# A chunked linear recurrence and a dense feed-forward layer in one kernel: the decay of C moves to the rows, three kinds of small matmuls get visits of their own, and GpSimd keeps the selects

## The chip, the core and the metric

The kernel runs on one core of a Trainium2 chip. The time is device microseconds of one execution. Several executions are timed, and the median is compared. A core has five engines with instruction queues of their own: PE (TensorE, matmuls, with weight loads listed as PEld), DVE (VectorE), ACT (ScalarE), POOL (GpSimd) and SP (SyncE, which issues the DMAs here). They meet through semaphores.

## The reference

Four batches, eight heads, 768 tokens, head dimension 32, state size 16. The first part is a recurrence over chunks with decay `a`, the second a two-matrix layer with a softplus between.

```python
for c in range(nc):                       # per chunk of tokens
    cum = np.cumsum(log_a[chunk], axis=-1)
    L = np.exp(cum[:, None] - cum[None, :]) * causal
    M = (Cc @ Bc.T) * L                   # scores
    y = M @ xc + (Cc @ state) * exp(cum)  # values + read
    state = exp(sum(la)) * state + sum_j Bc[j] * xc[j] * exp(cum[-1] - cum[j])
h = y @ w_in                              # (3072, 256) x (256, 2048)
g = softplus(h)
out = g @ w_out                           # (3072, 2048) x (2048, 256)
```

The weights arrive as 64-bit floats and are turned into 32-bit ones on the chip.

## The kernel before, in words

Tokens are taken in six rounds `r` of 128 tokens of each of the four batches, 512 columns in all. The six rounds of the recurrence feed the six column blocks `j` of the layer. All work is written out by hand: the string `ORDER` is a list of words, each of which emits the instructions of one step, and every engine keeps that order (`InOrder`). All instructions come through one helper, so the profile gives them one line, L141; they are told apart by their tiles.

The words of a round are these. `S` (scores) are 32 matmuls of B against C; a matmul of 32-bit data is two records, so 64 in the trace. `sel`, `rmp` (POOL) and `rm` (DVE) write the masked decay factors into `rm`; `M` multiplies the scores into it. `I` (values) is 64 matmuls, 128 records, of `rm` with x. `U` (updates, 64 records) makes the outer products for the state, `D`/`DD` keep their diagonal blocks in `zm`, `T` and `N` carry the state on. `R` (read, 64 records) adds C times state into the banks that `I` began. `G` (DVE) multiplies the result, in PSUM, by the growth tile `gg`, giving `y` in SBUF; `Xa` (ACT) rounds it to `xh`, `Yv`/`Yp` form the rest `xl`. `gg` of rounds 1 to 5 comes from DRAM (`gd`), each as four DMAs; that of round 0 is made on PE and ACT (`gs`, `ge`). `Bv`/`Bp` and `Cv`/`Cp` scale B and C by factors.

The layer's words are `F:j,k` (first matrix, six matmuls of 512 columns into bank 2 or 3), `s` (softplus, ACT, which empties that bank), `ha`/`hv`/`hp` (the rounded part `gh`, on ACT, DVE or POOL), `l` (the rest `gl`, DVE) and `Z:j,k` (second matrix, six matmuls). There are 96 `F` and 96 `Z`; I call either a block. Sixteen weight tiles `p` are loaded (`w:p`) and converted before they are needed: `Wg` (rebias, tile `w`), `Ws` or `Wsv` (sign), `Wb` and `Wo`, or `Wbv` and `Wo` (bits and word), `Wh` (high part), `Wl` (low part). Here `Wg`, and some of `Wh`, `Wl`, `h`, `T`, `N`, `B` and `C`, run on POOL.

Columns 0 and 1 are begun together: `F:0,0` starts when round 0 is through, round 1 and the weights are prepared beside the blocks of columns 0 and 1, and `F:2,0` follows round 2. From there a fixed pattern repeats, one round of the recurrence to one column. In it rounds 3 and 4 have one visit of PE, between `Z:j,6` and the next `F`:

```
F:2,10,2 Z:2,6 U:4,4,6 I:3,4,6,0,4 R:3,4,6,0,4 s:2,10 ha:2,10 l:2,10 F:2,11,3 Z:2,7 ...
```

and round 5, which has no `U` after it, `F:4,10,2 Z:4,6 I:5,4,6,0,4 R:5,4,6,0,4`. The DMAs are issued by SP in the same order; a DMA that waits holds back those after it.

## Time and profile before

| | us |
|---|---|
| timed runs, median (lowest to highest of 3) | 342.81 (341.96 to 346.05) |
| profiled execution, its own time | 344.31 |
| its span, first to last instruction | 342.6 |
| PE busy | 310.8 |
| DVE, ACT, POOL busy | 169.7, 135.5, 81.8 |
| mean granted clock of PE, share of full speed | 0.965 |

The span is what the views below are made of; 1.7 us of the execution's time lie outside it. A busy PE is a PE with matmuls under way, and records overlap, so that the time of a block is read from the distance of starts, not from durations.

### The profile page before, as it was taken

What the parts mean: (1) busy time and instruction counts of PE and PEld (TensorE: products, weight loads), DVE (VectorE), ACT (ScalarE), POOL (GpSimd) and SP (SyncE); (2) the same over time, 40 slices, a digit from 0 to 9 for tenths busy, and PEclk for the clock granted to TensorE, in tenths of its full rate; (3) what the DMA queues carried; (4) which work ended last, traced back from release to release, by engine and by line L of the source; (5) the groups of instructions that cost most, each with busy time, mean ns of one, the idle gap of its engine ahead of it and who ended that gap; (6) DMA issues with size and microseconds to landing.
All of it is one profiled execution on the core that took longest, in us unless ns stands there. A gap on an engine that the chain in (4) does not pass through costs nothing.

```text
span 342.6 us, 7297 instructions
## 1 busy us (share of the span) xinstructions
PE 310.8 (91%) x3148; PEld 253.8 (74%) x3148; DVE 169.7 (50%) x244; ACT 135.5 (40%) x228; POOL 81.8 (24%) x88
## 2 busy tenths in 40 slices
PE   5649879899799992999989999989999999999995
PEld 4538568678688781878868878868878888888884
DVE  4629979979796338336207325207335234232222
ACT  4625564323432212344415444405444434454440
POOL 5846972726712014500060000060000000000000
PEclk9958999999999998799989999989999999999999
DMA  7946323721540402041032031002010000010001
GB/s 228 388 174 186 104 87 120 279 66 58 231 106 2 146 11 61 0 138 51 0 97 61 3 121 65 0 4 61 2 61 2 0 4 1 0 61 3 0 0 61
DMA packets 14432, 26.05 MB, mean 76 GB/s; under 512 B 1088, under 2 KB 6976, under 8 KB 13760
## 3 DMA queue, kind: packets, MB, share of 16 engines
q1 hardware_dynamic: 14400, 25.60, 22.4%
q8 instruction: 24, 0.39, 0.5%
q14 instruction: 8, 0.07, 0.1%
HBM read 22.35 MB, written 3.24 MB: 75 GB/s over the span
## 4 chain that ended last, share of the span: by engine, by line
PE 77%; DVE 10%; issue 6%; POOL 3%; ACT 2%; DMA 1%; SPq 0%; DVEq 0%; ACTq 0%
PE banks L141 77%; DVE w L141 4%; DVE gl L141 2%; POOL w L141 1%; ACT e L141 1%; POOL xl L141 1%; DVE rm L141 1%; POOL cc L141 1%; DMA lr<-in_logs 1%; DVE s L141 1%; DVE y L141 0%; DVE zm L141 0%; ACT gh L141 0%; DVE bp L141 0%; ACT xh L141 0%
## 5 line engine op out<-in xcount | busy, mean ns | idle before, releaser
L141 DVE TENSOR_TENSOR gl<-e,gh 128x512 fp32r<-128x512 f32 x96 | 67.9, 716 | 136.7 <-ACT gh L141 129.6
L141 ACT ACTIVATE e<-banks 128x512 f32<-128x512 f32 x96 | 57.1, 597 | 110.1 <-PE banks L141 88.4
L141 PE MATMUL banks<-xh,wih 128*128 128x512 f32 (+1 forms) x196 | 78.9, 403 | 4.2 <-ACT xh L141 4.2
L141 PE MATMUL banks<-xl,wih 128*128 128x512 f32 (+1 forms) x196 | 77.7, 397 | 3.0 <-POOL xl L141 2.0
L141 PE MATMUL banks<-gh,woh 128*128 128x512 f32 (+1 forms) x196 | 76.9, 392 | 1.7 <-DVE half L141 1.7
L141 PE MATMUL banks<-xh,wil 128*128 128x512 f32 (+1 forms) x196 | 77.5, 395 | 0.0
L141 PE MATMUL banks<-gl,woh 128*128 128x512 f32 (+1 forms) x196 | 76.6, 391 | 0.8 <-DVE gl L141 0.8
L141 PE MATMUL banks<-gh,wol 128*128 128x512 f32 (+1 forms) x196 | 76.3, 389 | 0.6 <-DVE wol L141 0.6
L141 ACT CAST gh<-e 128x512 fp32r<-128x512 f32 x79 | 48.8, 619 | 52.3 <-PE banks L141 52.2
L141 POOL TENSOR_SCALAR_AFFINE_SELECT rm<-fc 64x1024 f32<-64x1024 f32 (+1 forms) x26 | 30.5, 1173 | 82.6 <-PE banks L141 81.5
L141 PEld LDWEIGHTS banks<-xh,wih 128*128 128x128 f32 x196 | 38.2, 195 | 13.2 <-ACT xh L141 4.6
L141 PEld LDWEIGHTS banks<-xl,wih 128*128 128x128 f32 x196 | 38.3, 196 | 10.7 <-POOL xl L141 2.3
L141 PEld LDWEIGHTS banks<-gh,woh 128*128 128x128 f32 x196 | 37.5, 192 | 10.0 <-DVE half L141 2.1
L141 PEld LDWEIGHTS banks<-gl,woh 128*128 128x128 f32 x196 | 37.5, 192 | 9.0 <-DVE gl L141 1.5
L141 PEld LDWEIGHTS banks<-xh,wil 128*128 128x128 f32 x196 | 38.2, 195 | 7.7
L141 PEld LDWEIGHTS banks<-gh,wol 128*128 128x128 f32 x196 | 37.5, 191 | 8.6 <-DVE wol L141 1.0
L141 POOL TENSOR_SCALAR w<-wraw 128x512 f32<-128x512 f32 x10 | 15.8, 1583 | 20.1 <-DVE wil L141 8.6
L141 DVE SCALAR_TENSOR_TENSOR w<-w,s 128x512 int32<-128x512 int32 x16 | 17.9, 1124 | 4.6 <-POOL w L141 4.1
L141 PE MATMUL banks<-rm,toks 64*32 64x64 f32 x768 | 10.2, 233 | 7.1 <-issue 5.3
L141 POOL CAST gh<-e 128x512 fp32r<-128x512 f32 x12 | 8.8, 743 | 28.9 <-PE banks L141 24.4
L141 DVE TENSOR_TENSOR rm<-banks,rm 128x1024 f32<-128x1024 f32 (+1 forms) x14 | 14.7, 1064 | 1.6 <-POOL rm L141 1.6
L141 PEld LDWEIGHTS banks<-rm,toks 64*32 64x32 f32 x768 | 8.6, 108 | 8.5 <-issue 6.1
(71 smaller groups left out, 192.4 us busy)
## 6 DMA issues: line engine op xcount, KB each, us to landing
rows<-in_rows SPq DMA_DIRECT2D x5, 1024.0 KB, 5.6
wraw<-in_w_in SPq DMA_DIRECT2D x8, 512.0 KB, 4.7
wraw<-in_w_out SPq DMA_DIRECT2D x8, 512.0 KB, 3.5
toks<-in_toks SPq DMA_DIRECT2D x5, 768.0 KB, 6.0
out_t<-half SPq DMA_DIRECT2D x11, 256.0 KB, 2.1
gg<-gd SPq DMA_DIRECT2D x20, 128.0 KB, 3.0
rows<-in_rows SPq DMA_DIRECT2D x1, 512.0 KB, 5.1
rows<-in_rows SPq DMA_DIRECT2D x2, 256.0 KB, 6.4
```

Of the source, the lines that this page charges most:

```text
L141: return lambda *a, **k: tc.keep_in_program_order(f(*a, **k))
```

## The change

The growth factor is applied to C, by rows, before the scores and the read, where it was applied to the result before. `gg` is now a tile of 128 rows (head and state) by 512, loaded by one DMA of 256 KB where four of 128 KB were; `cgv` multiplies C by it into `cg` (DVE), and `caa` (ACT) makes the two copies with every other head zeroed (`cap`), which came from DRAM before, so a round's rows are 512 KB where they were 1024 KB. `G` and `y` are gone: `Xa` and the new `Y` read PSUM, in two parts of 512. `S`, `I` and `R` stand apart in the pattern, with `U` beside `R`. GpSimd loses weights, `h`, `B` and `C` and keeps the selects and, in rounds 0 and 1 and once in 2, `T` and `N`. `warm` puts eight matmuls of zeros at the front. `lsp` spreads round 0's logarithms so that `gs` takes 4 matmuls where 32 were. `U` behind `I` in a bank doesn't start it anew. One more pair of `gh`/`gl` buffers is kept.

```diff
-B_AT, CAP_AT, C_AT, ROWS = 0, T, 3 * T, 4 * T
+B_AT, C_AT, ROWS = 0, T, 2 * T
...
+la kc0 some lr setup warm:8,1 kb w:0 to:0,2,3 ro:0,1,2 to:0,0,2 cla causal w:2 clr lla ro:0,0,1 keep llr fs:0,7 w:1
+lsp scan to:1 ts:0,6 fe:0,7 mid gs:0 ft:0,7 rmp:0,2,2,4 ow:0,6 Ws:0 rm:0,1,0,2 Bv:0 rs:0,6 ge:0 rmp:0,1,2,4 fs:1,7
+Wgv:0 re:0,6 Wb:0 cgv:0 ts:1,6 rmp:0,0,0,2 ow:1,6 caa:0,1 Wo:0 rs:1,6 rmp:0,3,0,2 re:1,6 Whv:0 caa:0,0 U:0,0,6,0
+Cv:0 elr Wlv:0 rmp:0,2,0,2 S:0,2,0,4 Ws:2 gd D:0,1,6 w:4 fe:1,7 D:0,0,0 ro:1 rmp:0,0,2,4 Wga:2 M:0,2,1,0,2 w:3
+ft:1,7 M:0,2,0,0,2 rmp:0,3,2,4 tl M:0,2,0,2,4 I:0,0,6,0,2 Tp:0,1 M:0,2,1,2,4 gg:1 Wb:2 R:0,0,6,0,2 Np:0,1 Wgv:1
+I:0,2,4,2,4 Xa:0,0,0,0,2 Xa:0,1,6,0,2 Y:0,0,0,0,2 R:0,2,4,2,4 Wb:1 rmp:1,3,0,4 Y:0,1,6,0,2 Wo:2 F:0,0,6,0,256
...
+Wlv:2 w:6 F:0,1,7,256,512 rmp:1,0,0,4 s:0,0 Wo:1 F:0,2,2 Ws:4 Bv:1 Wga:4 Tp:1,0 cgv:1 U:1,4,6,0 s:0,1 Wo:4
...
+hv:1,9 Cv:2 l:1,8 F:1,11,3 l:1,9 Z:0,15 s:1,11 I:2,4,6,0,4 to:4 E:0,0 E:0,1 hv:1,10 U:3,4,6,1 F:1,12,2 Z:1,8 s:1,12
...
+F:1,15,3 hv:1,14 l:1,12 Nv:3,0 Z:1,11 s:1,15 ha:1,15 R:2,4,6,0,4 Xa:2,1,6,0,4 Xv:2,0,4,0,4 Y:2,1,6,0,4 l:1,14 l:1,15
+Y:2,0,4,0,4 F:2,0,2 Z:1,12 s:2,0 ha:2,0 l:2,0 cgv:3 caa:3,0 caa:3,1 Cv:3 sel:3,0,0 sel:3,0,1 sel:3,1,0 sel:3,1,1
...
+F:2,4,2 Z:2,0 S:3,4,0,4 s:2,4 ha:2,4 l:2,4 M:3,4,0,0,4 gg:4 ro:4 F:2,5,3 Z:2,1 s:2,5 ha:2,5 l:2,5 M:3,4,1,0,4
+F:2,6,2 Z:2,2 s:2,6 ha:2,6 l:2,6 Bv:4 F:2,7,3 Z:2,3 s:2,7 ha:2,7 l:2,7 F:2,8,2 Z:2,4 I:3,4,6,0,4 s:2,8 ha:2,8 l:2,8
+F:2,9,3 Z:2,5 s:2,9 ha:2,9 l:2,9 F:2,10,2 Z:2,6 U:4,4,6,1 R:3,4,6,0,4 s:2,10 ha:2,10 l:2,10 Xa:3,0,4,0,4
...
+    def spread_logs():
+        A.activation(spread, la[:, NR * LA :].unsqueeze(2).broadcast_to([P, LA, N]), AF.Ln)
...
+    def grow_c(r, E):
+        cg = cg_s[r] = p2.tile([P, T], F32, tag="cg", name=f"cg{r}", bufs=1)
+        E.tensor_tensor(cg, rows(r)[:, C_AT:], growth_tile(r), op=ALU.mult)
+
+    def c_apart(r, e, E):
+        if r not in cap_s:
+            cap_s[r] = p2.tile([P, NB, 2, P], F32, tag="cap", name=f"cap{r}", bufs=1)
+        out, in_ = cap_s[r][:, :, e], cg_s[r].rearrange("p (b t) -> p b t", b=NB)
+        own = kb[:, K_BD + D * e : K_BD + D * e + 1]
+        if E is A:
+            A.activation(out, in_, AF.Copy, scale=own)
...
+        load(growth_tile(r), gd[:, r].unsqueeze(1).broadcast_to([NH, N, T]))
...
-                        start=v == 0,
+                        start=v == 0 and not behind,
...
+    def x_high(r, k, b, a, z, E):
+        copy(E, x_part(r, 0, k, a, z), y_part(b, a, z))
+
+    def x_low(r, k, b, a, z):
         V.tensor_tensor(
+            x_part(r, 1, k, a, z), y_part(b, a, z), x_part(r, 0, k, a, z).bitcast(F32), op=ALU.subtract
...
-XBUFS, WRAW, GBUFS = 2, 4, 4
+XBUFS, WRAW, GBUFS = 2, 4, 5
```

Of the kernel before, what the change touches and what calls it, by code (L numbers as in the profile page):

```python
# [54 lines left out]
Wlp:0 G:0,1,6,0,2 R:0,2,4,2,4 Xa:0,0,2 G:0,1,4,2,4 Wgp:2 G:0,0,2,2,4 Ws:2 Yv:0,0,2 sel:1,1,1 Xa:0,2,4 Wo:2
F:0,0,6,0,256 Wb:1 Yv:0,2,4 F:0,1,7,0,256 sel:1,1,0 Wha:2 w:5 Bv:1 F:0,0,6,256,512 w:6 Ws:4 Wlv:2 F:0,1,7,256,512
Wb:4 Wo:1 Wgp:4 F:0,2,2 s:0,0 Whv:1 sel:1,0,1 Wo:4 gg:1 s:0,1 U:1,4,6 s:0,2 Whv:4 F:0,3,3 ha:0,0 DD:1,4,6 Wlp:4
l:0,0 S:1,4,0,4 Tp:0,1 Wsv:6 Wga:6 Wlv:1 sel:1,0,0 ha:0,1 F:0,4,2 Wo:6 ha:0,2 Wbv:6 s:0,3 Cp:1 Z:0,0 Wb:3 l:0,1
M:1,4,1,0,4 ha:0,3 Np:0,1 F:0,5,3 Ws:3 Whp:6 M:1,4,0,0,4 Wga:3 Tp:1,0 Z:0,1 s:0,4 w:7 Np:1,0 Wo:3 w:8 I:1,4,6,0,4
Wlp:6 l:0,3 Wha:3 l:0,2 Wb:5 R:1,4,6,0,4 Wlp:3 ha:0,4 F:0,6,2 G:1,1,6,0,4 s:0,5 sel:2,0,0 Wga:5 G:1,0,4,0,4 Z:0,2  # L60
Ws:5 l:0,4 Wgp:8 Xa:1,0,4 w:9 Wo:5 F:0,7,3 hp:0,5 w:10 Wsv:7 Wha:5 Yv:1,0,4 s:0,6 Z:0,3 s:0,7 hp:0,6 Wlv:5 F:1,0,2
hv:0,7 Wga:7 some l:0,7 Z:0,4 l:0,6 l:0,5 F:1,1,3 Wo:7 s:1,0 Wbv:7 Z:0,5 Wsv:8 w:11 Wha:7 to:2 s:1,1 Wlv:7 ro:2
F:1,2,2 ha:1,0 Tv:1,1 Wgp:9 Wsv:9 l:1,0 Z:0,6 sel:2,1,0 s:1,2 Wo:9 ha:1,1 F:1,3,3 Wo:8 Np:1,1 Wbv:8 sel:2,0,1 Z:0,7
s:1,3 w:12 Bv:2 ha:1,2 l:1,1 U:2,4,6 K:0,1 hp:1,3 K:0,0 F:1,4,2 Wha:8 Tp:2,0 Wsv:11 Wbv:9 Z:1,0 l:1,2 w:13 Wsv:10
F:1,5,3 Whv:9 l:1,3 Z:1,1 DD:2,4,6 s:1,5 Wlv:9 s:1,4 S:2,4,0,4 Wlv:8 Nv:2,0 Wgp:10 F:1,6,2 hp:1,4 Wo:10 Z:1,2 Wbv:10
s:1,6 w:14 Wha:10 F:1,7,3 Wlv:10 Wsv:12 Wgp:12 Z:1,3 hv:1,5 Wgp:11 l:1,4 Wo:12 F:0,8,2 s:1,7 sel:2,1,1 l:1,5 ha:1,6
Z:1,4 Wbv:12 s:0,8 hp:1,7 Whv:12 Wsv:14 F:0,9,3 ha:0,8 Wo:11 l:1,6 Z:1,5 l:1,7 s:0,9 Wlv:12 F:0,10,2 hp:0,9 l:0,8
Cp:2 Wbv:11 Z:1,6 s:0,10 l:0,9 w:15 ro:3 to:3 Whp:11 gg:2 F:0,11,3 Wgp:14 Wlp:11 Z:1,7 Wo:14 s:0,11 ha:0,10 F:0,12,2
K:1,1 K:1,0 Wbv:14 Z:0,8 s:0,12 Wsv:13 Whv:14 Wga:13 l:0,10 F:0,13,3 ha:0,11 hv:0,12 Wlv:14 Z:0,9 s:0,13 l:0,11
# [56 lines left out]
def recurrence_then_ffn(ctx: ExitStack, tc: tile.TileContext, rows_in, toks_in, logs_in, w_in, w_out, const, outT):  # L126
# [199 lines left out]

    def load_growth(r):
        t = growth_tile(r)
        for h in range(4):
            load(  # L330
                t[h * D : h * D + D].rearrange("p g b t -> p (g b) t"),
                gd[h, :, r * P : r * P + P].unsqueeze(0).broadcast_to([D, 2 * NB, P]),
            )

    def growth_sums(g, b):
# [519 lines left out]
```

## Rows read from the trace of the kernel before

**Rows 1.** the page: busy time of each engine; PE's granted clock in 40 slices.

```profile
PE 310.8 (91%) x3148; PEld 253.8 (74%) x3148; DVE 169.7 (50%) x244; ACT 135.5 (40%) x228; POOL 81.8 (24%) x88
...
PEclk9958999999999998799989999989999999999999
```

**Rows 2.** busy time by stretch: width, each engine (instructions), PE's clock, DMA share, GB/s.

```profile
0.00:23.87 23.87, 13.71 (x372) 11.36 (x373) 9.53 (x21) 10.29 (x21) 14.37 (x32) 0.88 0.79 283
23.87:47.77 23.90, 19.06 (x384) 14.98 (x380) 20.93 (x23) 13.89 (x24) 18.87 (x16) 0.90 0.38 112
47.77:90.16 42.39, 40.69 (x300) 33.16 (x298) 38.15 (x53) 16.32 (x28) 23.21 (x21) 1.00 0.38 126
90.16:133.57 43.41, 37.03 (x401) 29.76 (x399) 26.37 (x40) 12.60 (x21) 7.11 (x9) 1.00 0.27 91
133.57:140.94 7.37, 5.35 (x12) 4.03 (x13) 4.11 (x3) 0.60 (x1) 7.15 (x5) 0.56 0.31 71
...
280.00:300.00 20.00, 20.00 (x90) 16.57 (x89) 7.50 (x12) 9.38 (x15) 0.00 (x0) 1.00 0.00 1
```

**Rows 3.** the chain that ended last, in order of time: start, length, what.

```profile
15.36 1.86 issue
...
19.42 3.45 issue
...
45.48 1.80 issue
...
132.47 1.05 ACT xh L141
...
133.60 2.44 POOL xl L141
...
224.42 1.62 issue
```

**Rows 4.** timeline of PE at round 3: start, length, instructions, [idle time before].

```profile
169.77 0.80 PE L141 MATMUL banks<-toks,bp 64*32 64x64 f32 x60
...
170.43 1.45 PE L141 MATMUL banks<-rm,toks 64*32 64x64 f32 x126
171.81 0.91 PE L141 MATMUL banks<-cc,st 32*64 32x64 f32 x44
174.27 0.56 PE L141 MATMUL banks<-cc,st 32*64 32x64 f32 x20 [1.55 <-issue]
```

**Rows 5.** busy time by stretch, as in Rows 2: rounds 3, 4 and 5, and after round 3.

```profile
169.77:179.21 9.44, 7.89 (x269) 6.65 (x269) 0.69 (x1) 1.22 (x2) 5.19 (x4) 0.82 0.29 88
176.00:178.00 2.00, 2.00 (x6) 1.52 (x6) 0.00 (x0) 0.60 (x1) 1.30 (x1) 0.50 0.00 0
221.47:230.97 9.50, 7.88 (x270) 6.68 (x269) 0.69 (x1) 1.22 (x2) 5.19 (x4) 0.82 0.02 3
...
273.22:278.57 5.35, 5.35 (x205) 4.71 (x205) 0.69 (x1) 1.22 (x2) 0.00 (x0) 1.00 0.01 3
```

**Rows 6.** the page, DMA queues: packets, MB, share of 16 engines.

```profile
q8 instruction: 24, 0.39, 0.5%
```

**Rows 7.** groups of DVE between 23.87 and 47.77: busy time, mean ns, idle.

```profile
L141 DVE SCALAR_TENSOR_TENSOR w<-w,s 128x512 int32<-128x512 int32 x5 | 6.3, 1256 | 0.6 <-POOL w L141 0.6
```

**Rows 8.** timeline of DVE.

```profile
28.81 0.68 DVE L141 SCALAR_TENSOR_TENSOR w<-w,s 128x512 int32<-128x512 int32 x1
...
53.62 0.43 DVE L141 CAST gh<-e 128x512 fp32r<-128x512 f32 x1 [0.22 <-PE banks L141]
```

**Rows 9.** groups of DVE between 180 and 220, POOL idle.

```profile
L141 DVE TENSOR_TENSOR gl<-e,gh 128x512 fp32r<-128x512 f32 x15 | 10.4, 692 | 29.2 <-ACT gh L141 29.2
```

**Rows 10.** DMA issues: KB each, median us to landing.

```profile
toks<-in_toks SPq DMA_DIRECT2D x1, 256.0 KB, 5.6
...
gd<-lr SPq DMA_DIRECT2D x1, 96.0 KB, 11.2
```

**Rows 11.** who waited for whom: us in total, times, longest.

```profile
POOL w L141 <- DMA wraw<-in_w_in: 2.2, 1, 2.2
```

More of the change, by code (lines that the diff above doesn't have):

```diff
@@ L55 @@
[L55 to L69, printed above, removed]
@@ new lines @@
+ft:1,7 M:0,2,0,0,2 rmp:0,3,2,4 tl M:0,2,0,2,4 I:0,0,6,0,2 Tp:0,1 M:0,2,1,2,4 gg:1 Wb:2 R:0,0,6,0,2 Np:0,1 Wgv:1
+I:0,2,4,2,4 Xa:0,0,0,0,2 Xa:0,1,6,0,2 Y:0,0,0,0,2 R:0,2,4,2,4 Wb:1 rmp:1,3,0,4 Y:0,1,6,0,2 Wo:2 F:0,0,6,0,256
+Xa:0,1,4,2,4 Xa:0,0,2,2,4 Y:0,1,4,2,4 F:0,1,7,0,256 Ws:1 rmp:1,2,0,4 Y:0,0,2,2,4 Whv:2 F:0,0,6,256,512 Wb:4 w:5
+Wlv:2 w:6 F:0,1,7,256,512 rmp:1,0,0,4 s:0,0 Wo:1 F:0,2,2 Ws:4 Bv:1 Wga:4 Tp:1,0 cgv:1 U:1,4,6,0 s:0,1 Wo:4
+rmp:1,1,0,4 caa:1,0 F:0,3,3 DD:1,4,6 caa:1,1 Whv:4 Np:1,0 s:0,2 Wlv:4 S:1,4,0,4 Tp:1,1 ha:0,0 Whv:1 Wlv:1 Wga:6
@@ new lines @@
+Ws:9 l:0,7 hv:1,0 s:1,2 F:1,3,3 l:1,1 Wga:9 l:1,0 ha:1,2 w:13 Z:0,7 Wo:9 Wb:10 F:1,4,2 K:0,1 K:0,0 s:1,3 Bv:2 Wb:11
+Z:1,0 cgv:2 Ws:10 Wlv:8 U:2,4,6,0 s:1,4 ha:1,4 F:1,5,3 l:1,4 l:1,2 Z:1,1 hv:1,3 s:1,5 l:1,3 F:1,6,2 Wga:10
+rm:2,2,0,4 w:14 Wo:10 Z:1,2 Whv:9 Wb:12 DD:2,4,6 F:1,7,3 caa:2,0 Wlv:9 Np:2,0 s:1,6 Whv:10 caa:2,1 Z:1,3 Wlv:10
+ha:1,5 rm:2,0,0,4 Wga:12 F:0,8,2 l:1,5 Wga:11 s:1,7 S:2,4,0,4 Ws:12 Z:1,4 ha:1,6 Ws:11 l:1,6 F:0,9,3 s:0,8 w:15
+Wo:11 ro:3 ha:1,7 to:3 gg:3 Z:1,5 l:1,7 s:0,9 Wb:13 hv:0,9 Wo:12 F:0,10,2 Ws:14 Z:1,6 Wha:12 s:0,10 Wlv:12 F:0,11,3
@@ L323, in growth_tile @@
         if r not in gg_s:
-            gg_s[r] = p2.tile([P, 2, NB, P], F32, tag="gg", name=f"gg{r}", bufs=1)
+            gg_s[r] = p2.tile([P, T], F32, tag="gg", name=f"gg{r}", bufs=1)
         return gg_s[r]
     def load_growth(r):
[L328 to L335, printed above, removed]
+        load(growth_tile(r), gd[:, r].unsqueeze(1).broadcast_to([NH, N, T]))
@@ L336, in growth_sums @@
+    def spread_logs():
+        A.activation(spread, la[:, NR * LA :].unsqueeze(2).broadcast_to([P, LA, N]), AF.Ln)
+    def growth_sums(b):
         sums = kc[:, : 2 * (P + SUB)].rearrange("p (c k) -> p c k", c=2)[:, :, :P]
         sums = sums.rearrange("p c (k i) -> p k c i", i=CH)[:, :, :, :SUB]
+        cols = spread.rearrange("p (b h) n -> p b (h n)", b=NB)
         for v in range(NB):
-            for hh in range(4):
-                at = (2 * g + hh // 2) * 2 * NB + 2 * v + hh % 2
-                PE.matmul(
-                    bank(b)[32 * hh : 32 * hh + 32, v * P : v * P + P].rearrange("p (k c i) -> p k c i", k=2, c=2),
-                    la[:, at : at + 1].broadcast_to([P, D]),
-                    sums,
-                    start=True,
-                    stop=True,
-                )
@@ L349, in growth_exp @@
-    def growth_exp(g, b, a, z):
-        A.activation(
-            growth_tile(0)[:, g, a:z], bank(b).rearrange("p (b t) -> p b t", b=NB)[:, a:z], AF.Exp, scale=-1.0
-        )
+            PE.matmul(
+                bank(b)[:, v * P : v * P + P].rearrange("p (k c i) -> p k c i", k=2, c=2),
+                cols[:, v],
+                sums,
+                start=True,
+                stop=True,
+            )
+    def growth_exp(b):
+        A.activation(growth_tile(0), bank(b), AF.Exp, scale=-1.0)
@@ L431, in scale_c, with updates @@
         cc = cc_s[r] = p2.tile([P, NB, 2, 2, SUB], F32, tag="cc", name=f"cc{r}", bufs=1)
-        src = rows(r)[:, C_AT:].rearrange("p (b k c i) -> p b k c i", k=2, c=2, i=SUB)
+        src = cg_s[r].rearrange("p (b k c i) -> p b k c i", k=2, c=2, i=SUB)
         f = row_factors(r)
-        for k in range(2) if r else (1,):
-            E.tensor_tensor(
-                cc[:, :, k],
-                src[:, :, k],
-                f[:, :, k, :2].unsqueeze(3).broadcast_to([P, NB, 2, SUB]),
-                op=ALU.mult,
-            )
-    def updates(r, b0, b1):
+        if r == 0:
+            out, src = cc[:, :, 1], src[:, :, 1]
+            f = f[:, :, 1, :2].unsqueeze(3).broadcast_to([P, NB, 2, SUB])
+        else:
+            out, src = (v.rearrange("p b k c i -> p (b k) c i") for v in (cc, src))
+            f = f.rearrange("p b k c -> p (b k) c")[:, :, :2].unsqueeze(3).broadcast_to([P, 2 * NB, 2, SUB])
+        E.tensor_tensor(out, src, f, op=ALU.mult)
+    def updates(r, b0, b1, behind):
         bp = bp_s[r]
@@ L763, in recurrence_then_ffn @@
         "Cp": lambda r: scale_c(r, Pl),
+        "cgv": lambda r: grow_c(r, V),
+        "cgp": lambda r: grow_c(r, Pl),
+        "cav": lambda r, e: c_apart(r, e, V),
+        "caa": lambda r, e: c_apart(r, e, A),
+        "cap": lambda r, e: c_apart(r, e, Pl),
         "U": updates,
@@ L822 @@
     br, cr = by_row(B), by_row(C)
-    apart = np.zeros((NR, P, NB, 2, P), C.dtype)
-    for h in range(NH):
-        hs = slice(h * N, h * N + N)
-        apart[:, hs, :, h % 2] = cr[:, hs]
     xt = x.reshape(NB, NH, NR, P, D).transpose(2, 3, 0, 1, 4).reshape(NR, P, -1)
@@ L829 @@
     arrays = {
[L830 removed]
+        "rows": c(np.concatenate([v.reshape(NR, P, -1) for v in (br, cr)], 2)),
         "toks": c(np.concatenate([xt, bt], 2)),
[L832 to L833 removed]
+        "alog": c(
+            np.concatenate(
                 [
                     a.reshape(NB, NQ, 2, NR, P).transpose(4, 3, 1, 0, 2).reshape(P, NR * LA),
[L836 to L837 removed]
+                    a[:, :, :P].transpose(2, 0, 1).reshape(P, LA),
+                ],
+                1,
             )
         ),
+        "alr": c(a.reshape(NB, NH, NR, P).transpose(1, 2, 0, 3).reshape(P, NR * LA)),
         "w_in": c(inputs["moe_w_in"]).view(np.int64),
```

142 lines of the change are left out of this document (60 added, 82 removed).

## Prediction

> **What bounds the kernel now.** I read the page first: PE is busy for 310.8 us of a span of 342.6, no other engine for half of it, and the granted clock is full except in a few slices [rows 1]. So the question is when PE stands still or runs slowly. The pattern late in the kernel gives its pace: 90 matmuls in 20.00 us, 0.222 us each, and so 1.33 us for a block of six [rows 2]. The 192 blocks would take 256 us. What is over lies in three places.
>
> First, PE reaches `F:0,0` only at 23.87 us. The chain of waits shows two pieces there in which PE waits for nothing that the profile shows, 1.86 and 3.45 us [rows 3], while the DMA engines are 0.79 busy [rows 2].
>
> Second, from 23.87 to 133.57, where `F:2,0` begins, there are 60 blocks (80 us) and nine visits of small matmuls (some 10 us), 90 us of work in 109.7. DVE is the other busy engine: 20.93 of 23.90 us and 38.15 of 42.39 [rows 2]. Before `F:2,0` the chain goes through ACT's `xh` and the rest `xl` on POOL, 2.44 us [rows 3], and the clock in the next 7.37 us is 0.56 [rows 2].
>
> Third, the visits of rounds 3 and 4. `U`, `I` and `R` run back to back, 256 matmuls; after the 44th of `R` PE stands for 1.55 us, in round 4 for 1.62 [rows 3, 4]. Then the clock falls to 0.50, the lower level of 1.2 GHz [rows 5]. Round 5, with `I` and `R` alone, has no idle time and clock 1.00 [rows 5].
>
> I read these gaps as instruction fetch. Queue 8 moved 24 packets of instructions, 0.39 MB, 16 KB each [rows 6]; PE has 2 x 3148 instructions [rows 1], 262 to a packet as an estimate. A round with its 32 blocks is 192 + 64 + 128 + 64 + 64 = 512 matmuls, 1024 instructions, four packets of 256: the gap must come back at the same matmul, and does. Small matmuls, 126 in 1.45 us [rows 4], use up a packet before the next is there; blocks, a packet in 128 x 0.222 = 28 us, do not.
>
> **The change part by part.** All terms are against the profiled execution, 344.31 us, 1.5 above the median.
>
> *Visits apart, rounds 3 to 5.* From the start of `U` to two blocks after `R` round 3 takes 9.44 us and round 4 9.50. Round 5 takes 5.35 without `U`, and `U` is 0.80 [rows 4, 5]: 6.15 undisturbed. So 3.29 + 3.35 = 6.64 us are gap and low clock. After the change no dense run there has over 128 matmuls (`I`; `U` with `R`), so a packet holds such a run and blocks besides. Counting the new order in steps of 256 instructions from the front (good to some 30), the steps fall near the middle of `I` and of `U`, and between two of them lie 48 instructions of blocks or more. Each extra visit costs a change of tile shape, which no row shows by itself; bounds zero and 0.44 (the 2.69 us of round 5's two visits, 5.35 less two blocks, minus 1.45 for `I` and 0.80 for a visit of 64), taken 0.2, three times. Sum -6.0, from -6.6 to -3.
>
> The Trainium skill, "Runtime: NRT & Kernel Launch", section "Instruction fetch mechanics", has the 16 KiB blocks of 256 instructions too, but holds that the fetch is mostly hidden, since dispatch is slower than the fill. By it the gap would have another cause and this term would be near 0. The row shows 1.55 us of unexplained idle time at a packet's end, so the measurement speaks against the page.
>
> *The front.* Before `F:0,0`, the growth sums fall from 64 records to 8, and `warm` adds 8, under the load of `la`, where PE has nothing else. Counted as above, one packet ends late in `U:0`, one near the end of the first `I`, one in `F:0,2`; of two gaps one can remain. The DMAs up to round 1's rows are some 1 MB less. New on the path are `cgv` on DVE and two `caa` on ACT ahead of `S`. No row shows `caa`: half of the 1.05 us of the 1024 wide `xh` [rows 3] and all of it are the ends, 0.6 taken, by width. DVE is what is late next. Its chain begins when the tokens of B land, 2.6 + 5.6 = 8.2 us [rows 10], with 14 instructions: `Bv`, `cgv`, `Wo`, `Wlv` and four `M` of 512 columns at 0.69 [rows 9], six copies and smaller ones at 0.43 [rows 8], 8.1 us; then 1.5 for selects in the way and hand-offs, and 1.3 for the last `xh` and `xl`, since `I` and `R` lie beside the last `M`: 19.1. Taken 19.0 against 23.87: -4.9. If the fetch holds the first `I` once more, 3.45 [rows 3] is the price and -1.4 is left; without hand-offs -6.4.
>
> *From `F:0,0` to `F:0,6`.* PE's work is 8 blocks, 10.7, and `U`, `S`, `I`, `R`, about 0.8 + 1.2 + 1.45 + 1.2: 15.3. DVE gets 25 instructions where 23 were. They now last 0.91 on average, and the word step 1.26, where the same step took 0.68 and a copy 0.43 at other moments [rows 2, 7, 8]; POOL is busy for 18.87 of these 23.90 us. With 0.69 or 0.43 they sum to 16.0, with 0.91 to 22.8. POOL keeps some 11 us of selects here, so I take 17; with 2 us for the slow clock of the first blocks, which stays (0.90 over 23.90 us now [rows 2]), 19.0 against 23.9. -4.9, from -7 to -1. The 1.80 us piece in round 1 [rows 3] goes with it: by the count no packet lies within `I:1 R:1`. `cgv:1` is a new wait on DVE, for `gg:1`, with `DD:1` and the weights `Whv:4` and `Wlv:4` behind it; `gd` took 11.2 us to land [rows 10], behind 6.4 MB, and is now issued behind 3.9. I cost it at nothing; as late as before it would cost 4.
>
> *From there to `F:0,12`.* 28 blocks and two visits, 39.3, take 42.39 [rows 2]. DVE drops from 38.15 to 31 to 37, but ACT rises from 16.32 to some 35, most of it weights that POOL had. I keep 2.5 us of stalls: -0.6, from -2 to +3.
>
> *From `F:0,12` to `F:2,0`.* 24 blocks and three visits, 35.5, take 43.41. `I:2` and `U:3` now stand side by side, 192 matmuls, and by the count one packet lies wholly within: a gap of about 1.95 (128 small matmuls take 1.5 us; 128 back from 174.27 lies at 170.9, so that packet lasted 3.4 [rows 4]). `R:2` moves to the end, so PE waits for one `Xa`, 1.0; hand-offs 1.0. 39.4: -4.0, from -6 to 0.
>
> *`F:2,0` and `Z:1,12`.* 7.37 now. `xl` now comes from DVE in `Y`, `l`, `l`, `Y`, four of 0.69, 2.8 after `Xv`, instead of 2.44 on POOL, but the idle time ahead is shorter; I keep a low clock of 3 us. 6.9: -0.5, from -3 to +1.
>
> *Costed at nothing.* From `F:2,0` the new `cgv` (0.69) and two `caa` lie beside 32 blocks, 43 us, of which DVE and ACT fill under half (7.50 and 9.38 of 20.00 us [rows 2]). `G`, two of 0.69, goes from DVE. If that cover were gone, 3 x 1.9 us. The buffer pair more and `U`'s start flag add no instruction.
>
> Sum: -6.0 - 4.9 - 4.9 - 0.6 - 4.0 - 0.5 = -20.9; 344.31 - 20.9 = 323.4 in a profiled execution, and 342.81 - 20.9 = 321.9, say 322, as a median.
>
> **The rivals.**
>
> *The early gains are eaten.* Weights go to and fro between ACT and DVE, each of which waits in order for the other; DVE stays the bound at 0.91 each. For it: DVE at 90% before. Against: the sums above stay under PE's work. Half of the front and of the fourth term remain and none of the second and third: 342.81 - 2.4 - 2.0 - 0.5 - 6.0 = 331.9.
>
> *The gaps are not fetch*, or come back elsewhere. Then the 1.55 and 1.62 us and the slow clock stay: 321.9 + 6.0 = 328. Against: their return after exactly four packets. The page of the Trainium skill cited above comes to this case.
>
> *Weights on ACT stop PE: slower.* ACT empties the two banks of `F`. If a weight step waits at the head of ACT's queue for its load, `s` waits behind it, and PE two blocks later. POOL waited so once, for 2.2 us [rows 11], and nobody felt it. If each of the 15 tiles after the first did, 33 us: 321.9 + 33 = 355. It decides from 20.9 / 15 = 1.4 us a tile. Against: one such wait in the trace, and loads issued far ahead.
>
> *The change doesn't do what it says.* Round 2's visits do not stand apart, as told; and if the selects alone hold DVE at 0.91, the second term falls to -1: 326, within the first case's range.
>
> **How the numbers follow.** The forecast, with the last case, 0.68; early gains eaten, 0.20, of which a quarter misses 2%; gaps stay, 0.07; slower, 0.04; the rest beyond all bounds. Low ends of the terms together (-6.6, -6.4, -7, -2, -6, -3) would give 312, which asks for all at once: low end 313. The first rival, with 3 us for an odd wait, gives 335, the high end. 2% of the median, about what a measurement of this kernel tells from no change, is 6.9 us, so faster is under 335.9 and slower over 349.7. Faster 0.87, within 0.09, slower 0.04.
>
> **What would show it.** Right: no idle piece of over 1 us in PE after `F:2,0`'s first blocks, clock 1.00 from there, `F:0,0` near 19 us, the word step near 0.7, `F:2,0` near 119 us, one gap in `U:3`. Wrong: pieces without a releaser in `I` or `R` of rounds 3 to 5; PE waiting for ACT's `e` between 45 and 90 us; `cgv:1` waiting for its DMA; `F:0,0` after 22 us.

## The result, and the profile after

The changed kernel takes 319.3 us in the median (318.34 to 320.14, 4 runs) against 344.43 for the kernel before on the same chip (341.96 to 346.18, 4 runs): ratio 0.927 [0.920, 0.935]. The forecast was 322, between 313 and 335. The profiled execution took 319.96 us, its span is 318.2: against the 344.31 and 342.6 of before, 24.4 us less where the terms summed to 20.9.

The page of the changed kernel, with the lines that answer to [rows 1, 6]:

```profile
PE 306.1 (96%) x3100; PEld 249.3 (78%) x3100; DVE 159.1 (50%) x249; ACT 157.5 (49%) x269; POOL 46.1 (14%) x62
...
PEclk9979999999999997999999999999999999999999
...
q8 instruction: 24, 0.39, 0.5%
```

PE is busy for 4.7 us less, but the span is 24.4 us shorter: PE's idle time fell from 31.8 to 12.1 us. What PE waited for says which part went (total us, times, longest), first before, then after:

```profile
PE banks L141 <- issue: 10.7, 6, 3.5
PE banks L141 <- ACT xh L141: 4.2, 1, 4.2
```

```profile
PE banks L143 <- DVE rm L143: 2.1, 1, 2.1
PE banks L143 <- DVE xl L143: 2.0, 1, 2.0
...
PE banks L143 <- issue: 0.5, 2, 0.3
```

The pieces of [rows 3] for which the profile showed no releaser have gone, those at the front and in round 1 as well as those in rounds 3 and 4; the two that are left are of 0.28 and 0.17 us. The work by stretch, cut where the prediction cut it (columns as in [rows 2]; the last two are rounds 3 and 4 from `U` on, `U`, `R` and two blocks, without the `I` that is in [rows 5]):

```profile
0.00:18.97 18.97, 15.06 (x324) 11.33 (x324) 11.95 (x26) 12.05 (x23) 13.66 (x35) 0.95 0.88 297
18.97:37.90 18.93, 17.21 (x385) 14.01 (x381) 18.28 (x25) 13.14 (x23) 12.95 (x14) 0.96 0.25 80
37.90:78.51 40.61, 40.61 (x302) 33.14 (x297) 30.47 (x53) 30.12 (x53) 2.90 (x3) 1.00 0.59 193
78.51:116.00 37.49, 36.53 (x402) 29.80 (x400) 24.56 (x42) 15.54 (x28) 5.52 (x4) 1.00 0.13 36
116.00:122.45 6.45, 4.48 (x13) 3.31 (x14) 3.43 (x6) 1.21 (x2) 0.00 (x0) 0.77 0.00 0
122.45:318.20 195.75, 192.25 (x1689) 157.68 (x1687) 70.43 (x101) 85.43 (x142) 11.04 (x8) 1.00 0.08 27
...
152.90:157.80 4.90, 4.90 (x142) 4.16 (x142) 1.98 (x3) 2.37 (x5) 0.25 (x1) 1.00 0.01 3
201.50:206.40 4.90, 4.90 (x142) 4.12 (x142) 1.98 (x3) 2.37 (x5) 0.28 (x1) 1.00 0.02 3
```

From `F:0,6` (37.90) to `F:0,12` (78.51) PE is never idle. The last stretch has the same 1689 matmuls as before, in 195.75 us instead of 201.66. The chain, in order of time:

```profile
1.41 5.03 PE banks L143 x14
...
6.76 1.79 POOL rm L143
...
31.28 70.77 PE banks L143 x655
102.04 0.17 issue
102.21 13.04 PE banks L143 x156
...
115.28 0.59 ACT xh L143
...
115.89 0.69 DVE xl L143
116.58 1.20 DVE gl L143 x2
117.78 0.61 DVE xl L143
...
118.44 190.34 PE banks L143 x1522
```

One piece of 190 us of PE ends the kernel almost without a break. In front of it stands the last hand-off that costs something, `xh` and two `xl` with two `gl` between them, as in [rows 3] but with DVE in POOL's place. Timelines of the changed kernel: the eight `warm` matmuls and the first of the log sums, the one issue gap that is left inside a run of small matmuls, and two DVE steps beside the selects.

```profile
1.41 3.59 PE L143 MATMUL banks<-small 128*32 128x512 bf16 x8 [1.41 <-DVE small L143]
4.93 1.28 PE L143 MATMUL banks<-la,kc 128*128 128x32 f32 x5
...
101.65 0.40 PE L143 MATMUL banks<-toks,bp 64*32 64x64 f32 x14
102.21 0.71 PE L143 MATMUL banks<-toks,bp 64*32 64x64 f32 x46 [0.17 <-issue]
...
21.65 1.20 DVE L143 SCALAR_TENSOR_TENSOR w<-w,s 128x512 int32<-128x512 int32 x1
...
26.04 0.68 DVE L143 TENSOR_TENSOR zm<-banks,kb 128x512 f32<-128x512 f32 x1
```

Groups over the whole span (busy, mean ns, idle before them): the word step, which had a mean of 1124 ns over the whole span before and has one of 917 in the stretch where [rows 7] has 1256, and the two new operations.

```profile
L143 DVE SCALAR_TENSOR_TENSOR w<-w,s 128x512 int32<-128x512 int32 x16 | 11.9, 743 | 0.7 <-ACT s L143 0.6
L143 DVE TENSOR_TENSOR cg<-rows,gg 128x512 f32<-128x512 f32 x6 | 4.7, 791 | 3.1 <-DMA gg<-gd 2.0 <-ACT gg L143 1.0
L143 ACT ACTIVATE cap<-cg,kb 128x512 f32<-128x512 f32 x12 | 8.2, 715 | 4.9 <-DVE cg L143 4.8
```

### The profile page after: what moved, and what is told of

It is laid out like the page before. It is cut to its first block, busy times and chain, and to the rows that moved or that the text cites. A ratio compares the mean times of both kernels' runs of the same rounds, so it can differ in the third digit from the quotient of the medians.

```text
span 318.2 us, 7119 instructions
## 1 busy us (share of the span) xinstructions
PE 306.1 (96%) x3100; PEld 249.3 (78%) x3100; DVE 159.1 (50%) x249; ACT 157.5 (49%) x269; POOL 46.1 (14%) x62
## 4 chain that ended last, share of the span: by engine, by line
PE 90%; DVE 5%; POOL 2%; issue 1%; ACT 1%
PE banks L143 90%; POOL rm L143 2%; DVE gl L143 1%; DVE wil L143 1%; DVE xl L143 1%; DVE rm L143 0%; DVE bp L143 0%; DVE w L143 0%; DVE cg L143 0%; ACT xh L143 0%; DVE woh L143 0%; DVE wih L143 0%; ACT gh L143 0%; DVE zm L143 0%; ACT half L143 0%
## 5 line engine op out<-in xcount | busy, mean ns | idle before, releaser
L143 DVE TENSOR_TENSOR gl<-e,gh 128x512 fp32r<-128x512 f32 x96 | 68.8, 722 | 121.7 <-ACT gh L143 121.6
L143 PE MATMUL banks<-xh,wih 128*128 128x512 f32 (+1 forms) x196 | 77.8, 397 | 0.8 <-ACT xh L143 0.8
L143 PE MATMUL banks<-xl,wih 128*128 128x512 f32 (+1 forms) x196 | 76.0, 388 | 2.0 <-DVE xl L143 2.0
L143 PE MATMUL banks<-xh,wil 128*128 128x512 f32 (+1 forms) x196 | 76.0, 388 | 0.0
L143 POOL TENSOR_SCALAR_AFFINE_SELECT rm<-fc 64x256 f32<-64x256 f32 (+2 forms) x36 | 36.0, 1000 | 130.3 <-PE banks L143 125.8
L143 ACT CAST gh<-e 128x512 fp32r<-128x512 f32 x83 | 51.2, 617 | 2.1
L143 PEld LDWEIGHTS banks<-xl,wih 128*128 128x128 f32 x196 | 37.3, 190 | 9.1 <-DVE xl L143 2.3
L143 PEld LDWEIGHTS banks<-xh,wil 128*128 128x128 f32 x196 | 37.1, 189 | 7.6
L143 ACT ACTIVATE s<-wraw 128x512 f16<-128x512 f32 (+1 forms) x32 | 24.7, 787 | 4.4 <-DVE w L143 2.7
L143 DVE SCALAR_TENSOR_TENSOR w<-w,s 128x512 int32<-128x512 int32 x16 | 11.9, 743 | 0.7 <-ACT s L143 0.6
L143 DVE TENSOR_TENSOR xl<-banks,xh 128x512 fp32r<-128x512 f32 (+1 forms) x14 | 8.2, 611 | 5.4 <-ACT xh L143 5.3
```

What stands on the lines that cost most here:

```text
L143: return lambda *a, **k: tc.keep_in_program_order(f(*a, **k))
```

## The experiments

A word list below is the part of `ORDER` that differs. Times are medians, ratios are to the kernel before on the same chip.

**The changed kernel again**, with no edit, to set the later ones beside; below it is a0.

> The changed kernel itself once more, as the mark for the runs beside it. Both theories: ratio to before 0.927 or a little above; 317 to 321 us.

320.97 us (319.99 to 321.52, 6 runs), ratio 0.935 [0.930, 0.939]; `F:0,0` at 19.63, `F:2,1` at 123.30, span 318.8. `U:3` has no gap in this trace. Five traces have the front of the changed kernel unaltered (its own, this one, and those of the joined visits, the early read and the doubled growth below), and `F:0,0` is at 18.97, 19.63, 18.60, 19.39 and 18.05 us in them: a difference of up to 1.6 us at the front shows nothing.

**The visits joined again.** `I:3` and `I:4` go back beside `U` and `R`; nothing else differs from the changed kernel.

```diff
-F:2,8,2 Z:2,4 I:3,4,6,0,4 s:2,8 ... Z:2,6 U:4,4,6,1 R:3,4,6,0,4
+F:2,8,2 Z:2,4 s:2,8 ... Z:2,6 I:3,4,6,0,4 U:4,4,6,1 R:3,4,6,0,4   (round 4 alike)
```

> The changed kernel with one thing undone: in rounds 3 and 4 the values stand beside U and R again, one run of 256 small matmuls. Fetch theory: PE runs dry at a packet's end inside the run; counted along the order the end falls near the 28th matmul of U, with the packet's start some 57 instructions into the run, so the gap is between the 0.17 us of round 2's run in the changed kernel (36 in) and the 1.55 of round 3 before (216 in), say 0.5 to 1.3 us, in both rounds at the same matmul; with a low clock behind it or not, 1 to 5 us over the changed kernel's 319.3. Rival, that the length of the visit alone brings the idle time and the low clock: gap of 1.5 us in R as before, 6 to 6.7 us over. Rival, that the visits are not what was gained: within 0.5 us of 319.3.

324.38 us (323.15 to 328.11, 4 runs), ratio 0.950 [0.945, 0.954]; span 321.8. PE's timeline in round 3:

```profile
151.76 1.48 PE L141 MATMUL banks<-rm,toks 64*32 64x64 f32 x128
153.04 0.48 PE L141 MATMUL banks<-toks,bp 64*32 64x64 f32 x29
155.38 0.57 PE L141 MATMUL banks<-toks,bp 64*32 64x64 f32 x35 [1.86 <-issue]
```

The gap is back, within `U` where the packets were counted to end, 1.86 us here and 1.56 in round 4, longer than the 0.5 to 1.3 expected. `F:2,1` comes at the same time (122.43 against 122.45); the 3.6 us more of span are these gaps. The clock stays at 1.00 after both, so the second half of the old price didn't come back.

**The same, with the packets moved.** 32 small zero matmuls at the front move every later instruction by 64 (matmul and weight load) against the ends of the packets.

```diff
+pad:32,1        # ahead of kb
+    def pad(n, b):
+        for _ in range(n):
+            PE.matmul(bank(b)[:32, :2], some, some[:, :2], start=True, stop=True)
```

> As the joined visits, with 32 matmuls of two columns at the very front, 64 instructions, so that every packet ends 32 matmuls earlier in the work. Fetch theory: the gap leaves U and comes near the 60th matmul of R, 96 matmuls later, in rounds 3 and 4, with 1.4 to 1.7 us since the packet then lies wholly inside the run; a new gap of 1 to 1.8 us comes at the end of round 1's R, whose run now holds a whole packet, and the one in U:3 of round 2 goes. Rival, gaps that belong to the visit: same matmul and same length as without the 32, none in round 1. The front may come 1 to 2 us later by the added matmuls.

334.22 us (one run), span 332.5. Round 3:

```profile
162.48 0.85 PE L141 MATMUL banks<-toks,bp 64*32 64x64 f32 x64
163.26 1.15 PE L141 MATMUL banks<-cc,st 32*64 32x64 f32 x61
165.93 0.33 PE L141 MATMUL banks<-cc,st 32*64 32x64 f32 x3 [1.53 <-issue]
```

In the run of `I`, `U` and `R`, 256 matmuls, packets ended after 29 and 157 in the version above; 32 matmuls earlier, and one packet of 128 on, that is 125 and 253. The gap moved from 157 to 253, 64 + 61 after `I`: each time to the end of the packet that lies wholly in the run. In round 4 it is 1.43 us. The gap in `U:3` has gone, and new ones stand in round 1 (1.70 us) and at the front:

```profile
24.29 0.49 PE L141 MATMUL banks<-cc,zm 32*64 32x64 f32 x7 [4.06 <-issue]
```

`F:0,0` is at 24.70 us with it, 5 to 6.7 us later than in the five traces above, where 1 to 2 were expected. Instructions that compute nothing moved the gaps: they belong to a place in the instruction stream, not to operands. Here the clock did fall after round 3 (0.50 from 167 to 169 us), not after round 4.

**The visits apart in the kernel before.**

```diff
-F:2,10,2 Z:2,6 U:4,4,6 I:3,4,6,0,4 R:3,4,6,0,4
+F:2,8,2 Z:2,4 I:3,4,6,0,4 ... F:2,10,2 Z:2,6 U:4,4,6,1 R:3,4,6,0,4   (rounds 4, 5 alike)
-                        start=v == 0,
+                        start=v == 0 and not behind,
```

> The kernel before with this part of the change alone: in rounds 3 to 5 the values go four blocks ahead of U and R (U without the flag that starts the bank). Fetch theory: no idle time of PE and clock 1.00 in both rounds, -6.0 us by the prediction's term, so 338.4 against 344.4, ratio 0.982; round 1's gap of 1.8 us stays. Rival, gaps of another cause: they stay, ratio 1.00, or more by 0.6 us for three more changes of tile shape.

338.72 us (337.76 to 340.82, 10 runs), ratio 0.9925 [0.989, 0.996]. From `F:2,1` on, as a stretch:

```profile
141.25:336.90 195.65, 192.08 (x1689) 157.61 (x1687) 70.99 (x105) 81.81 (x134) 11.74 (x9) 1.00 0.11 35
```

195.65 us, the changed kernel's length to 0.1 us, and 6.0 less than the profiled execution of before. The median fell by only 3.2 us (the interval of the ratio allows 1.5 to 3.7), about the two gaps alone (1.55 + 1.62). The low clock stood behind both gaps in the execution that the forecast was read from; in the traces of two versions below that keep these visits joined (the rebias steps off GpSimd, the hand-off in the kernel before) it stands behind one of two.

**The rebias steps back on GpSimd.** In the changed kernel, 15 of the 16 go to POOL.

```diff
-Wga:2 ... Wgv:1 ... Wga:4 ... Wga:6   (15 words)
+Wgp:2 ... Wgp:1 ... Wgp:4 ... Wgp:6
```

> The changed kernel with the rebias of 15 weight tiles on GpSimd again (one step of six for each tile; the rest as changed). Theory that GpSimd's work stretches DVE and that this reaches PE: the word step on DVE goes from a mean of 0.74 us to 1.0 or more, PE waits again for gl, w or wol between 38 and 80 us, 2 to 4 us over 319.3. Rival, that DVE has cover enough and ACT and DVE are relieved of 15 steps of 0.4 to 0.7 us: the step is stretched, but PE has no new waits, within 0.7 us of 319.3.

326.15 us (324.55 to 326.62, 4 runs), ratio 0.955 [0.951, 0.959]. The first three stretches, and one of DVE's waits:

```profile
0.00:20.51 20.51, 15.25 (x324) 11.50 (x324) 11.57 (x25) 11.33 (x22) 15.68 (x36) 0.93 0.85 289
20.51:41.91 21.40, 19.53 (x384) 16.19 (x381) 18.47 (x23) 11.69 (x21) 19.21 (x18) 0.83 0.20 62
41.91:84.02 42.11, 41.71 (x303) 32.83 (x297) 33.44 (x53) 26.68 (x46) 17.09 (x12) 1.00 0.55 184
```

```profile
DVE w L141 <- POOL w L141: 5.1, 3, 2.2
```

They are 1.5, 2.5 and 1.5 us longer than the changed kernel's. The first ends 0.9 us after the latest of the five fronts above, and the second ran at clock 0.83 instead of 0.96. The median is 6.9 us over 319.3, more than the 2 to 4 expected. The word step has a mean of 746 ns, as with the steps on ACT (743), but only three of its 16 ran beside a rebias step. Other steps of DVE did get longer there: of the twelve `gl` that ran beside one, five took 1.02 to 1.15 us instead of 0.69. One of them, and the rebias steps beside it:

```profile
50.90 1.12 DVE L141 TENSOR_TENSOR gl<-e,gh 128x512 fp32r<-128x512 f32 x1
...
49.06 3.29 POOL L141 TENSOR_SCALAR w<-wraw 128x512 f32<-128x512 f32 x2 [2.94 <-DVE wol L141]
```

Over all 96 `gl` that is 1.3 us (70.1 against 68.8 of busy time). The larger part is that DVE waits for the rebias steps, 5.1 us, as it did for 4.1 in the kernel before. So the price was too low and the step that was named was the wrong one.

**The rebias steps off GpSimd in the kernel before.**

```diff
-Wgp:0 ... Wgp:1 ... Wgp:2 ... Wgp:4   (10 words)
+Wga:0 ... Wga:1 ... Wga:2 ... Wga:4
```

> The kernel before with the ten rebias steps of GpSimd on ACT and nothing else. Theory that GpSimd's rebias (1.58 us each) held the weights back: DVE's waits for POOL's w (4.1 us) go, PE's waits between 24 and 93 us shrink, 2 to 5 us under before. Rival, that this needed the new order around it: within 1 us of before, or over it where ACT's steps now wait in the wrong place.

338.07 us (335.82 to 340.14, 6 runs), ratio 0.986 [0.982, 0.991], 5.35 us less. Two of its stretches:

```profile
24.09:47.39 23.30, 19.63 (x385) 15.70 (x381) 19.63 (x23) 14.52 (x25) 15.89 (x15) 0.85 0.38 115
...
89.64:131.13 41.49, 36.73 (x401) 29.83 (x399) 23.12 (x39) 12.57 (x21) 5.38 (x7) 0.99 0.22 69
```

In the profiled execution 3.2 us lie ahead of `F:2,1`, most in the second of these (43.41 before). In the first PE is idle for 3.7 us instead of 4.8, but at clock 0.85 instead of 0.90, and 0.6 us is won; the word step's mean is 883 ns, where it was 1124. Another 1.9 us lie behind `F:2,1`, where the edit changes nothing and the clock fell once instead of twice. So this part alone is worth about 3 us, and up to 5 by the median.

**The hand-off before `F:2,0`, in the kernel before.** Scaling, `xh` and `xl` of round 2 move ahead of the last `l` steps.

```diff
-l:1,14 l:1,15 G:2,0,4,0,4 G:2,1,6,0,4 Xa:2,0,4 DD:3,4,6 ... gg:3 Yp:2,0,4
+l:1,10 G:2,0,4,0,4 G:2,1,6,0,4 Xa:2,0,4 Yp:2,0,4 ... l:1,14 l:1,15 DD:3,4,6 ... gg:3
```

> The kernel before with one thing of the order: round 2's two G, its Xa and Yp go up, from the last place before F:2,0 to behind l:1,10. From Z:1,11 to F:2,1 the kernel before takes 13.11 us, of which three blocks and a change of shape are 4.2. Theory that this was the place in DVE's order and not the growth scaling: no idle piece there, 8 us under before. Rival, that G and xl on GpSimd are too slow in any place: 4 us under or less.

338.04 us (335.19 to 339.31, 4 runs), ratio 0.985 [0.979, 0.990], 5.4 us less and not 8. `F:2,0` starts 1.2 us later (134.73), but not by the edit: the stretch from `F:0,6` to `F:0,12`, which ends ahead of the first word that was moved, took 3.2 us more in this execution, at a lower clock (42.39 and 1.00 in [rows 2]). That stretch, and the two that hold the edit, with what PE still waits for in them:

```profile
48.07:93.64 45.57, 43.87 (x299) 35.42 (x297) 37.65 (x53) 16.28 (x28) 23.85 (x21) 0.93 0.35 117
93.64:134.73 41.09, 37.35 (x402) 29.68 (x400) 25.70 (x35) 11.92 (x21) 9.14 (x10) 1.00 0.33 110
134.73:137.60 2.87, 2.87 (x12) 2.36 (x13) 2.24 (x2) 1.20 (x2) 2.81 (x3) 1.00 0.00 0
...
132.93 0.50 PE L140 MATMUL banks<-gl,woh 128*128 128x512 f32 x1 [1.44 <-DVE gl L140]
```

From `F:0,12` to `F:2,0` it took 41.09 us instead of 43.41, and from there to `F:2,1` 2.87 instead of 7.37: 6.8 us of the 8, all by the order. A block ahead of `F:2,0` now waits 1.44 us for `gl`.

**The same in the changed kernel.** `R:2` and all of its hand-off stand one `F` and one `Z` earlier.

```diff
-Z:1,11 s:1,15 ha:1,15 R:2,4,6,0,4 Xa:2,1,6,0,4 Xv:2,0,4,0,4 Y:2,1,6,0,4 l:1,14 l:1,15 Y:2,0,4,0,4
+l:1,13 R:2,4,6,0,4 Xa:2,1,6,0,4 Xv:2,0,4,0,4 Y:2,1,6,0,4 Y:2,0,4,0,4 F:1,15,3 ... l:1,14 l:1,15
```

> The changed kernel with round 2's read and the two X and two Y steps moved up, from the last place before F:2,0 to behind Z:1,10, with F:1,15 and Z:1,11 to cover them. From R:2 to F:2,1 the changed kernel takes 8.40 us, of which the read is 1.09 and two blocks 2.72. Theory that PE waits there for X and Y and that the low clock (0.50) follows from that idle time: no idle piece over 0.3 us, clock 1.00, 4.4 us under the changed kernel. Rival, that DVE is then late with gl for Z:1,8 to Z:1,11 (1.9 us of X and Y ahead of them in its order): half of it, 2 us under. Rival, that the clock falls there anyway from the small matmuls: 2.5 us under.

315.70 us (314.73 to 318.56, 6 runs), ratio 0.921 [0.916, 0.925]: 5.3 us under a0.

```profile
115.84:118.56 2.72, 2.72 (x14) 2.25 (x12) 1.74 (x4) 2.35 (x4) 0.00 (x0) 1.00 0.00 0
118.56:314.10 195.54, 191.98 (x1689) 157.51 (x1687) 71.44 (x102) 85.42 (x143) 11.04 (x8) 1.00 0.08 27
```

`F:2,0` to `F:2,1` in 2.72 us (a0: 6.66), no idle time, no low clock: a version that beats both kernels. Ahead of it, from `F:0,12` to `F:2,0`, another 0.75 us went.

**Growth on C done twice** in rounds 3 to 5, to test that it is hidden.

```diff
-cgv:3 caa:3,0 caa:3,1
+cgv:3 cgv:3 caa:3,0 caa:3,0 caa:3,1 caa:3,1   (rounds 4, 5 alike)
```

> The changed kernel with the growth of C and its two copies done twice in rounds 3 to 5 (the second result is used). The prediction costed these steps at nothing, beside 32 blocks, and at 1.9 us a round without that cover. Theory: within 0.3 us of the changed kernel. Rival, that they reach PE through the in-order queues of ACT and DVE: up to 5.7 us over it.

320.99 us (318.59 to 322.83, 4 runs), ratio 0.935 [0.928, 0.941], a0's time. In the trace it is not quite nothing: in rounds 3 to 5 PE waits once for ACT's `e`, which stands behind the four `caa`, and the stretch takes 0.27 us more (`F:3,1` to `F:3,4`: 8.43 us here, 8.16 in a0):

```profile
172.33 0.19 PEld L142 LDWEIGHTS banks<-xh,wih 128*128 128x128 f32 x1 [0.39 <-ACT e L142]
```

So the rival's path exists, at 0.3 us a round for the doubled steps where it had 1.9.

**No `warm`.**

```diff
-setup warm:8,1 kb w:0
+setup kb w:0
```

> The changed kernel without the eight warm matmuls at the front. The prediction costed them at nothing, under the load of la. The trace after shows them for 3.59 us, to 5.0, and the factor sums behind them at 4.93, while the logarithms are done at 3.48; the chain then runs through GpSimd's selects from 6.76 on. Theory that they lie on that chain: F:0,0 1.0 to 1.4 us earlier, 1 to 1.4 us under the changed kernel. Rival, that they buy PE a faster clock at the front: factor sums, growth sums and scores longer, 0 to 2 us over it. Rival, that selects or loads set the front anyway: within 0.3.

323.19 us (319.94 to 325.81, 6 runs), ratio 0.939 [0.933, 0.946], whose interval overlaps a0's. The log sums start at 3.78 us instead of 4.93; `F:0,0` is at 19.15, inside the spread of the unaltered front. But 16 instructions fewer move the packets, and in `U:3`:

```profile
102.01 0.46 PE L141 MATMUL banks<-toks,bp 64*32 64x64 f32 x22
104.07 0.64 PE L141 MATMUL banks<-toks,bp 64*32 64x64 f32 x38 [1.60 <-issue]
```

The gap, of 0.17 us or none, has become 1.60, eight matmuls later in `U`. The profiled execution has a span of 318.3 all the same, because its clock stayed at 1.00 behind `F:2,0`: from there to `F:2,1` it took 5.08 us where a0 took 6.66.

**`warm` with two columns.** As many instructions, no length.

```diff
-warm:8,1
+pad:8,1
```

> The changed kernel with the eight warm matmuls cut from 512 columns to 2: the same count of instructions, so the same packets, without their 3.6 us. Without them at all round 2's gap went from 0.2 to 1.6 us and the whole was 2.2 us slower. Theory that this was the packets' place: the gap in U:3 is at its 18th matmul again with under 0.6 us, the front starts 1 us earlier, 320 us, 0.5 to 1 under the changed kernel. Rival, that the warm matmuls hold the clock up: 323, as without them.

320.19 us (317.83 to 321.64, 6 runs), ratio 0.934 [0.929, 0.938]; `F:0,0` at 18.70, again inside the spread, `U:3` without its 1.60 us gap. So the gap in `U:3` went by the number of instructions and not by what `warm` does for the clock.

**All of it:** the early `R:2`, `U:3` two blocks further from `I:2`, no `warm`.

```diff
-setup warm:8,1 kb w:0
+setup kb w:0
-hv:1,10 U:3,4,6,1 F:1,12,2 Z:1,8
+hv:1,10 F:1,12,2 Z:1,8 U:3,4,6,1   (R:2 as above)
```

> Round 2's read early as before, round 3's U taken away from round 2's values to behind Z:1,8, and no warm matmuls. With fetch as the cause of the gap in U:3, it goes whatever the alignment; the front comes 0.5 to 1.1 us earlier. 314.5 us, 1 to 1.5 under the run with the early read alone (315.7), ratio to before 0.916. Rival, that one more visit costs what the gap did: 315.5 to 316.

315.84 us (314.85 to 316.43, 6 runs), ratio 0.921 [0.917, 0.924]. No gap in `U:3`, but the early `R:2` alone had none there either, and it is no faster. Without `warm` a gap of 1.07 us stands in the first `I` (0.32 in the early `R:2`), and `F:0,0` is at 19.08.

## Why the prediction was right, point by point

| step, from the start of the first to that of the second | forecast | measured |
|---|---|---|
| begin to `F:0,0` | -4.9 | -4.90 |
| `F:0,0` to `F:0,6` | -4.9 | -4.97 |
| `F:0,6` to `F:0,12` | -0.6 | -1.78 |
| `F:0,12` to `F:2,0` | -4.0 | -5.92 |
| `F:2,0` to `F:2,1` | -0.5 | -0.92 |
| `F:2,1` to the end | -6.0 | -5.91 |

**The visits.** Right, by every test: joined they give the gap back, the gap moves with the packets, and apart in the kernel before they take away 6.0 of 6.0 us of its profiled execution. "Rival: the gaps are not fetch" is refuted by the 64 empty instructions. Two things in the traces bear it out further. Wherever PE stops for over 0.3 us without a releaser inside a run of small matmuls, in any of the versions, the number of matmuls before the stop leaves 88 to 93 when divided by 128 (221, 349, 732, 1242, 1753, 1880, 2392 and others), whichever matmul stands there. And the packets of queue 8 are timed: for each of the 16 such stops of over 1.3 us behind `F:0,0`, a packet of 16 KB starts 0.7 to 1.3 us after the matmul 128 places earlier and takes 0.9 to 1.6 us, and PE goes on 0.9 to 1.7 us after it has landed (round 3 before: 170.84, 171.57 to 172.90, 174.27). From one place to the next that is 3.1 to 3.7 us, where 128 small matmuls take 1.5.

The Trainium skill, "Runtime: NRT & Kernel Launch", section "Instruction fetch mechanics", holds that crossing a 16 KiB boundary is mostly hidden; here it is so beside blocks, and not in a run of small matmuls (up to 1.86 us), so for such runs the measurement decides. One thing was wrong: the low clock was taken as a sure part of the price. The gaps alone are about 3 us and are in every trace of the kernel before that keeps the visits joined; the low clock, about 3 more where it follows both, stands behind four of the six gaps there. So the term was worth some 3 to 6 us.

**The front.** The right number, and in part by luck: the same front ends between 18.05 and 19.63 us in five traces, -4.2 to -5.8, and the path was wrong. The chain was to run through DVE from the tokens; in the trace after it runs through `warm`, the log sums and POOL's selects (6.76 to 14.29 us). In a0 it runs through PE until 8.62, then ACT's `gg` and DVE's `cg`: two paths of nearly one length. So `warm`, costed at nothing, "under the load of `la`", is on both chains, with eight matmuls until 5.00 us; that its length costs time at `F:0,0` is not shown, since 18.70 with two columns and 19.15 without it lie within the spread.

What was right there is the count of the packets: of the two gaps, after matmul 221 and 349, "one can remain", and the one in the first `I` remains with none to 0.67 us, while the other falls to `F:0,2` and costs 0.46 us at most. The two were 5.31 us before, more than the whole gain. The run with 32 empty matmuls shows the part of their place: matmul 349 lies in the last visit again, the gap is 4.06 us and `F:0,0` at 24.70. So having 48 records fewer ahead of it (56 fewer of the growth sums, eight more of `warm`) helped by moving a packet's end out of the last visit; that the shorter work helped besides is not shown.

**`F:0,0` to `F:0,6`.** Sum right. The reason, that POOL's work beside DVE makes DVE's steps longer, holds for the selects (the word step 1.20 us beside them, where it takes 0.68 alone; `zm`, with one operand in PSUM, keeps its 0.68 beside a select) and in part for the rebias steps, whose larger price is that DVE waits for them. The Trainium skill, "SBUF — State Buffer", section "SBUF: two separate sides", has one pair of ports that DVE, with two inputs in SBUF, and GpSimd take from each other for a whole instruction; the rows agree that a conflict exists. Whether a whole select is waited for they don't tell, since a select too is longer beside such a step (1.05 to 1.08 us, where one beside `xl` took 0.73). DVE is busy for 18.28 of these 18.93 us, where 17 were forecast, so it may still set their end; the gains were not eaten all the same. The new wait of `cgv:1` for its load was costed at nothing, and it is nothing; `cgv:2` waits 2.0 us, in the next stretch, where PE is never idle.

**The third and fourth terms** were mis-sized, 1.2 and 1.9 us too small. I kept 2.5 us of stalls in the third, and PE is never idle (40.61 us against 39.3 of work as summed): ACT rose to 30.12 us and still holds nothing up, which also refutes the rival of weights on ACT that stop PE. In the fourth I took 1.95 us for the gap in `U:3`, 1.0 for `Xa` and 1.0 for hand-offs; the gap is 0.17, and none to 0.33 in the other six traces with the packets in this place. The place was forecast and only its size missed: eight matmuls away it is 1.60. How much the place in the order is worth by itself shows in the kernel before: moving round 2's hand-off alone takes away 6.8 us from `F:0,12` to `F:2,1`, as much as the whole change does there (6.84).

**`F:2,0`.** The low clock stays, as kept (0.77 over 6.45 us), though not in every run: in two traces with the same order here (no `warm`, growth done twice) the clock is 1.00 and the stretch takes 5.08 and 5.05 us. The early `R:2` shows it is all order: 3.2 to 4.7 us from `F:0,12` to `F:2,1` were left on the table, depending on whether the clock falls.

**Costed at nothing** from `F:2,0` on: shown, by doing it twice, to within 0.3 us a round.

**The chances.** Those of the cases under 335.9 us (0.68, three quarters of 0.20, and 0.07) add up to 0.90, not to the 0.87 that is stated for faster.

Of 24.4 us the runs so far place: visits 6.0 (the gaps' 3 in every trace), the front's two gaps up to 5, the rebias steps 3 in the kernel before and 6.7 in the changed one, the hand-off before `F:2,0` 6.8 in the one and 3.2 to 4.7 still open in the other. They overlap and don't add up; what the growth on C by itself gave early on was not tried alone.
